# Attention, mixture of experts and feed-forward in one program: the low halves of the first expert's weights computed on VectorE instead of GpSimd

## The chip, the cores and the metric

One core of one Trainium2 chip runs the whole program in one launch. The metric is the device time of that launch in microseconds. The median of three runs of the kernel before is 1288.56 us, the lowest 1285.17 and the highest 1292.94.

## What is computed

Three stages follow each other, each on the output of the one before. Of the reference, shortened:

```python
def _attn_ref(x, state):                  # x (8, 8, 512, 64), state (8, 8, 32, 64)
    xread = softmax(scale * np.matmul(x, state.transpose(0, 1, 3, 2))) @ state
    sread = softmax(scale * np.matmul(state, x.transpose(0, 1, 3, 2))) @ x
    return np.concatenate([xread, sread], axis=2)
def _moe_ref(x, expert_emb, tau, w1, w2): # w1 (8, 512, 1024), w2 (8, 1024, 512)
    expert_idx = np.argmax(xn @ en.T / tau, axis=1)   # rows and embeddings of length one
    for e in range(E):
        mask = expert_idx == e
        h = np.maximum(x[mask] @ w1[e], 0.0)
        out[mask] = gate_w[mask, None] * (h @ w2[e])
def _moe2_ref(x, w_in, w_out, alpha):     # w_in (512, 2048), w_out (2048, 512)
    h = x @ w_in
    g = np.maximum(h, 0.0) + alpha * np.minimum(h, 0.0)
    return g @ w_out
```

Between the stages there are 4352 rows of 512 values: 8 batches of 512 tokens and 32 states.

## The kernel before

All large products after the attention are made with f16 operands in two halves: a matrix v is scaled by a power of two, its high half is v rounded to f16, and its low half is what is left, rounded to f16. A product is then three matmuls: high by high, low by high, high by low. So before the experts' loop starts, the first expert's w1 and w2 must be loaded as f32 (into `st1` and `st2`), measured (sums of squares), scaled, and split into `w1h`, `w1l`, `w2h`, `w2l`.

This is done beside the attention. The attention runs in 16 **units** (k = 0 to 15), one for each batch b and each half g of its heads, written out in order in one Python loop. The order of the instructions on each engine is the order in which this loop records them; nothing reorders it. In unit k:

- TensorE transposes the row maxima (`u_m1T`, line 358), subtracts the maxima (`u_E2T`, line 368), makes the scores of the next unit (`u_S`, line 321), then the products of the states' reading (`u_sread`, line 384), the transposed scores of the next unit (`u_Sn`, line 341), and the products of the tokens' reading (`xr_mm`, line 416), two PSUM tiles of 128 x 584 values.
- ScalarE copies and exponentiates (lines 324, 360, 370, 376), and sums squares.
- VectorE takes the maximum for the next unit (`u_m2`, line 330), scales the states' reading (`u_sr`, lines 395 to 397), reduces the maxima (`u_m1`, lines 350 to 352), does side work that is spread over the units (`put_rows`, line 543: two or three 128 x 128 instructions per unit from unit 7 on; `e_onehot`, lines 492 to 499; `e_scale`, lines 473 to 476), and at the end normalizes the two PSUM tiles (`xr_dve`, lines 436 to 452).
- GpSimd makes a diagonal matrix of the maxima (lines 331 to 334).
- SyncE issues the loads and stores, in order.

The two tiles that line 416 writes have two buffers, so line 384 of a unit waits for the instructions of line 448 of the unit before.

The splitting of the weights hangs on this loop as **tasks**: `tasks[k]` is run near the end of unit k, just after `xr_dve` and one instruction of each chain in `later`. `cv_task(i, c)` splits quarter c of w1 (i = 0, in units 6, 7, 8, 9) or of w2 (i = 1, in units 11, 12, 13, 14), 128 x 1024 values each. Its high half is one ScalarE instruction (`split_hi`, line 130). Its low half is, in the kernel before, four GpSimd instructions: for each of two 512-wide pieces a multiplication by the scale `a_w[i]`, in place in `st1` or `st2` (line 687), and a subtraction (line 688). The later experts' low halves, in the experts' loop, are made by VectorE (`convert`, which calls `split_lo`, line 133).

In unit 14 GpSimd also issues the first two gathers of rows for the experts (`early_load`, line 584), and in unit 15 ScalarE and VectorE split these rows (`early_prep`, lines 130 and 133).

Of the kernel before, what the change touches and what calls it, by code (L numbers as in the profile page):

```python
# [14 lines left out]
ALU = mybir.AluOpType  # L15
# [7 lines left out]
def tile_attn_moe_ffn(ctx, tc, x, xt, state, statet, embt, tau, w1, w2, w_in, w_out, alpha, out):  # L23


    nc = tc.nc
# [71 lines left out]
    a_w = [const.tile([128, 1], F32, name=f"a_w{i}") for i in range(4)]  # L98
# [30 lines left out]
    def split_hi(hi, src, sc):  # L129
        nc.scalar.activation(out=hi, in_=src, func=AF.Copy, scale=sc)  # L130

    def split_lo(lo, hi, src, sc):
        nc.vector.scalar_tensor_tensor(out=lo, in0=src, scalar=sc, in1=hi, op0=ALU.mult, op1=ALU.subtract)  # L133
# [11 lines left out]
    def decode_ops(dst, d):  # L145
# [9 lines left out]
    W = {  # L155
        0: (st1.rearrange("p (c k) f -> p c (k f)", c=4), w1h.rearrange("p (c k) f -> p c (k f)", c=4),
            w1l.rearrange("p (c k) f -> p c (k f)", c=4)),
        1: (st2.rearrange("p (c k) f -> p c (k f)", c=4), w2h.rearrange("p (c k) f -> p c (k f)", c=4),
            w2l.rearrange("p (c k) f -> p c (k f)", c=4)),
    }  # L160
# [41 lines left out]
    def attention(st, pA, pST, pXr):  # L202
# [479 lines left out]
        def cv_task(i, c):  # L682
            def f():
                split_hi(W[i][1][:, c, :], W[i][0][:, c, :], a_w[i])
                for q in range(2):
                    src, hi, lo = (v[:, c, q * 512:(q + 1) * 512] for v in W[i])
                    nc.gpsimd.tensor_tensor(src, src, a_w[i].to_broadcast([128, 512]), ALU.mult)
                    nc.gpsimd.tensor_tensor(lo, src, hi, ALU.subtract)
            return f

        tasks = {k: [] for k in range(2 * B)}
# [33 lines left out]
        for k, (b, g) in enumerate(units):  # L725
# [70 lines left out]
            if k in scales:  # L796
                i = scales[k]
                norm_sum(spare[1][:, 0:4], fsq[i])
                tot = sm.tile([128, 1], F32, tag="sc_t", name="sc_t")
                v = sm.tile([128, 1], I32, tag="sc_v", name="sc_v")  # L800
# [50 lines left out]
        c = B - 1  # L851
# [727 lines left out]
```

## Time and profile before

| | |
|---|---|
| median of 3 runs | 1288.56 us (1285.17 to 1292.94) |
| time of the profiled execution | 1292.34 us |
| its span, first to last instruction | 1290.6 us |
| mean granted TensorE clock | 0.977 of full speed |
| attention (units 0 to 15) | about the first 140 us |
| experts' loop | to about 600 us |
| feed-forward | the rest |

The profile lists five engines: PE is TensorE, DVE VectorE, ACT ScalarE, POOL GpSimd, SP SyncE. A group of instructions is named by source line, engine and operation, what it writes, and what it reads. In a timeline a row begins with the start in us from the span's start and the duration; several like instructions in a row are merged, with their number behind x; in brackets stands how long the engine sat idle before, and which instruction ended that.

### The profile page before, as it was taken

To read this page: it belongs to the slowest core of one execution; us is meant where nothing else is said; L and a number is where in the kernel's file an instruction comes from. 1 tells how busy PE (TensorE), PEld (TensorE's weight loads), DVE (VectorE), ACT (ScalarE), POOL (GpSimd) and SP (SyncE) were. 2 spreads that over 40 slices of the span, in tenths; PEclk is the share of its full clock that TensorE was granted. 3 is DMA by queue.
4 is the path that set the end of the run, shared out by engine and by line. 5 is a ranking of instruction groups with operands and counts; after the bars stand their busy time and mean duration, and the time that the engine had idled before them with its cause. 6 is when DMAs were issued, how large, how long until landed. Compare 5 with 4: busy or idle time off the path is not lost.

```text
span 1290.6 us, 21097 instructions
## 1 busy us (share of the span) xinstructions
PE 1205.5 (93%) x7520; PEld 687.5 (53%) x7520; DVE 810.2 (63%) x1640; ACT 566.1 (44%) x1045; POOL 360.0 (28%) x421
## 2 busy tenths in 40 slices
PE   9887889998888897988999999999999999999997
PEld 5555434443333343333446666666666666666664
DVE  5888856756687776565898555546455454645543
ACT  5955532235484635353555334333343333333343
POOL 2345445554446544454201011020110201001010
PEclk9988989999999998998999999999999999999999
DMA  9884767899999989985102010020101102000000
GB/s 290 273 274 147 208 156 188 185 203 245 205 265 217 274 211 216 181 210 106 38 1 50 18 33 34 2 58 9 34 33 24 43 1 41 25 18 34 1 25 26
DMA packets 221648, 148.48 MB, mean 115 GB/s; under 512 B 174014, under 2 KB 190526, under 8 KB 220480
## 3 DMA queue, kind: packets, MB, share of 16 engines
q1 hardware_dynamic: 210976, 117.30, 38.0%
q0 software_dynamic: 10240, 29.49, 7.5%
q8 instruction: 61, 1.00, 0.3%
q14 instruction: 83, 0.68, 0.2%
q10 hardware_dynamic: 288, 0.02, 0.0%
HBM read 80.13 MB, written 28.40 MB: 84 GB/s over the span
## 4 chain that ended last, share of the span: by engine, by line
PE 52%; DMA 1%; DVE 0%; issue 0%; ACT 0%; POOLq 0%; DVEq 0%
PE bk L1395 27%; PE pm L1449 12%; PE bk L1449 9%; PE bk L1411 2%; PE pm L1411 1%; DMA hT<-hs 1%; PE yp L1066 1%; DMA out_dram<-arena,fr 0%; POOLq L1575 0%; DVE ys L133 0%; DVE arena L1455 0%; DVE ym L1073 0%; ACT arena L1400 0%; ACT ys L130 0%; ACT arena L1368 0%
## 5 line engine op out<-in xcount | busy, mean ns | idle before, releaser
L1395 PE MATMUL bk<-woh,arena 128*128 128x512 f16 x1088 | 399.8, 379 | 0.0
L1395 PEld LDWEIGHTS <-arena 128*128 128x128 f16 x1632 | 158.1, 98 | 100.2
L1395 PE MATMUL bk<-wol,arena 128*128 128x512 f16 x544 | 206.2, 379 | 0.0
L1455 DVE SCALAR_TENSOR_TENSOR arena<-bk,sg,arena 128x256 f32<-128x256 f32 (+1 forms) x128 | 59.7, 466 | 215.4 <-PE bk L1449 215.0
L1457 ACT ACTIVATE arena<-pm,sg 128x256 f32<-128x256 f32 (+1 forms) x192 | 88.4, 461 | 195.6 <-PE pm L1449 194.9
L1066 PE MATMUL yp<-w2h,hT 128*128 128x512 f16 x576 | 140.6, 400 | 29.7 <-DMA hT<-hs 21.4
L1066 PEld LDWEIGHTS <-hT 128*128 128x128 f16 x864 | 83.4, 100 | 138.9 <-DMA hT<-hs 33.9
L1368 ACT CAST arena<-arena 128x512 f16<-128x512 f32 (+1 forms) x144 | 85.1, 591 | 157.8 <-DVE arena L1373 157.4
L1053 PE MATMUL hp<-w1h,xTt 128*128 128x512 f16 x576 | 133.5, 382 | 19.6 <-DMA xTt<-xs 13.4
L1053 PEld LDWEIGHTS <-xTt 128*128 128x128 f16 x864 | 84.5, 98 | 126.1 <-DMA xTt<-xs 15.8
L1284 POOL DMA_INDIRECT gt<-gate_d,fr x34 | 34.3, 1010 | 393.8 <-DMA fr<-y_nat 327.0
L1449 PEld LDWEIGHTS <-wS 128*128 128x128 f16 x1152 | 108.3, 98 | 50.6 <-issue 0.2
L1449 PEld LDWEIGHTS <-winh 128*128 128x128 f16 x1024 | 98.6, 98 | 64.5 <-issue 0.8
L1373 DVE SCALAR_TENSOR_TENSOR arena<-arena,alpha_sb 128x512 f32<-128x512 f32 (+1 forms) x144 | 102.7, 714 | 3.2 <-ACT arena L1415 3.1
L1372 DVE TENSOR_TENSOR arena<-arena 128x512 f16<-128x512 f32 (+1 forms) x144 | 94.0, 658 | 16.1 <-ACT arena L1368 15.1
L130 ACT ACTIVATE ys<-yp,ym 128x512 f16<-128x512 f32 x38 | 26.0, 684 | 172.2 <-DVE ym L1075 155.3
L1449 PE MATMUL pm<-ysum,wS 128*128 128x256 f16 (+1 forms) x768 | 99.6, 266 | 0.1
L1086 POOL DMA_INDIRECT y_nat<-ys,pos x38 | 39.5, 1040 | 209.7 <-issue 151.0
L1295 POOL DMA_INDIRECT out_dram<-arena,fr x34 | 34.7, 1022 | 205.3 <-ACT arena L1400 140.3
L1449 PE MATMUL bk<-yT,winh 128*128 128x256 f16 (+1 forms) x512 | 86.5, 266 | 0.0
L1053 PE MATMUL hp<-w1l,xTt 128*128 128x512 f16 x288 | 68.4, 379 | 0.1
L164 ACT ACTIVATE junk<-st 128x1024 bf16<-128x1024 f32 x56 | 59.2, 1056 | 21.2 <-SPq L1100 8.2
(318 smaller groups left out, 1938.0 us busy)
## 6 DMA issues: line engine op xcount, KB each, us to landing
st<-in_w_dram SPq DMA_DIRECT2D x64, 512.0 KB, 5.8
X<-in_x_dram SPq DMA_DIRECT2D x32, 256.0 KB, 8.8
d<-in_w_in_dram SPq DMA_DIRECT2D x8, 1024.0 KB, 5.6
d<-in_w_out_dram SPq DMA_DIRECT2D x8, 1024.0 KB, 5.4
xs_all<-xrow SPq DMA_DIRECT2D x7, 1056.0 KB, 6.5
xT<-in_xt_dram SPq DMA_DIRECT2D x7, 1024.0 KB, 6.4
xs_all<-xrow SPq DMA_DIRECT2D x2, 528.0 KB, 4.0
xT<-in_xt_dram SPq DMA_DIRECT2D x2, 512.0 KB
```

Of the source, the lines that this page charges most:

```text
L164: nc.scalar.activation(out=junk, in_=W[i][0][:, c, :], func=AF.Square, accum_out=fsq[i][:, c:c + 1])
L1053: nc.tensor.matmul(hp[s][c], lhsT=xTt[s][:, q + k, :], rhs=wt[:, k, c * 512:(c + 1) * 512], start=(i == 0 and k == 0), stop=(i == 2 and k ...
L1066: nc.tensor.matmul(yp[s], lhsT=hT[s][:, q + k, :], rhs=wt[:, k, :], start=(i == 0 and k == 0), stop=(i == 2 and k == KE - 1))
L1086: nc.gpsimd.indirect_dma_start(out=y_nat[:], out_offset=bass.IndirectOffsetOnAxis(ap=pos[:, s:s + 1], axis=0), in_=ys[:].bitcast(I32), in_ ...
L1368: nc.scalar.copy(slot[G[g, m]][:, 0, 0:n], h)
L1372: tt(d[:, 1, 0:n], h, d[:, 0, 0:n], sub)
L1373: return [lambda: nc.vector.scalar_tensor_tensor(h, in0=h, scalar=alpha_sb[:, m:m + 1], in1=h, op0=ALU.mult, op1=ALU.max), hi, lo]
L1395: nc.tensor.matmul(ps, lhsT=slot[G[g, m]][:, lg, t * 128:(t + 1) * 128], rhs=wo[lw][:, m, :], start=(m == order[0] and i == 0), stop=(m == ...
L1411: nc.tensor.matmul(ps, lhsT=wi[l][:, k, m * 128:(m + 1) * 128], rhs=yT[0][:, y + k, :], start=(n == 0), stop=(n == 11))
L1449: nc.tensor.matmul(ps, lhsT=a, rhs=b, start=(i in (1, 2, 5) and j == 0), stop=(j == len(ops) - 1), skip_group_check=True)
L1455: nc.vector.scalar_tensor_tensor(d, in0=ps, scalar=sc, in1=d, op0=ALU.mult, op1=add)
L1457: nc.scalar.activation(out=d, in_=ps, func=AF.Copy, scale=sc)
```

## The change

The four GpSimd instructions of a task give way to one call of `split_lo`, that is one VectorE `scalar_tensor_tensor` over 128 x 1024 values: src times a_w minus hi, written as f16. The staging tiles are no longer scaled in place.

```diff
         def cv_task(i, c):
             def f():
                 split_hi(W[i][1][:, c, :], W[i][0][:, c, :], a_w[i])
-                for q in range(2):
-                    src, hi, lo = (v[:, c, q * 512:(q + 1) * 512] for v in W[i])
-                    nc.gpsimd.tensor_tensor(src, src, a_w[i].to_broadcast([128, 512]), ALU.mult)
-                    nc.gpsimd.tensor_tensor(lo, src, hi, ALU.subtract)
+                split_lo(W[i][2][:, c, :], W[i][1][:, c, :], W[i][0][:, c, :], a_w[i])
             return f
```

Lines below the change move up by three in the file after it.

On VectorE, at the end of unit 9 and the start of unit 10, the order before is this (`xrow`, `lg`: what `xr_dve` writes; `sc_t` to `inv_w`: the scale of w2, a chain in `later`; `m`: the next unit's maximum):

```order
L448 TENSOR_TENSOR lg<-xr,zz 128x64
L436 TENSOR_TENSOR xrow_150<-xr,zz 128x512
L448 TENSOR_TENSOR lg<-xr,zz 128x64
L174 TENSOR_REDUCE sc_t<-xr 128x1
L175 TENSOR_SCALAR sc_v<-sc_t 128x1
L176 TENSOR_SCALAR a_w_106<-sc_v 128x1
L802 RECIPROCAL inv_w_112<-a_w_106 128x1
L330 TENSOR_REDUCE m_1263<-pST 128x1
L395 TENSOR_SCALAR rz_1301<-xr 128x1
```

and with the change this:

```order
L448 TENSOR_TENSOR lg<-xr,zz 128x64
L436 TENSOR_TENSOR xrow_150<-xr,zz 128x512
L448 TENSOR_TENSOR lg<-xr,zz 128x64
L174 TENSOR_REDUCE sc_t<-xr 128x1
L133 SCALAR_TENSOR_TENSOR w1l<-st_122,a_w_105,w1h 128x1024
L175 TENSOR_SCALAR sc_v<-sc_t 128x1
L176 TENSOR_SCALAR a_w_106<-sc_v 128x1
L799 RECIPROCAL inv_w_112<-a_w_106 128x1
L330 TENSOR_REDUCE m_1251<-pST 128x1
L395 TENSOR_SCALAR rz_1289<-xr 128x1
```

The new instruction stands behind the two line 448 instructions and ahead of the next unit's maximum (line 330) and of line 395. There are eight such places, one in each of the units 6 to 9 and 11 to 14.

On GpSimd, in units 6 to 8, the order before is this (`m2b`, `dg`: the diagonal of the maxima):

```order
L331 CAST m2b<-m_964 128x1
L332 TENSOR_TENSOR m2b<-m_964,m2b 128x1
L334 AFFINE_SELECT dg<-m2b 128x256
L687 TENSOR_TENSOR st_122<-st_122,a_w_105 128x512
L688 TENSOR_TENSOR w1l<-st_122,w1h 128x512
L687 TENSOR_TENSOR st_122<-st_122,a_w_105 128x512
L688 TENSOR_TENSOR w1l<-st_122,w1h 128x512
L331 CAST m2b<-m_1055 128x1
```

and with the change this:

```order
L331 CAST m2b<-m_961 128x1
L332 TENSOR_TENSOR m2b<-m_961,m2b 128x1
L334 AFFINE_SELECT dg<-m2b 128x256
L331 CAST m2b<-m_1049 128x1
```

All 32 instructions of lines 687 and 688 are gone from GpSimd; between two units only the three instructions of the diagonal are left.

## Rows read from the trace of the kernel before

**Rows 1.** The page, part 1: busy time, share of the span, instructions of each engine.
```profile
PE 1205.5 (93%) x7520; PEld 687.5 (53%) x7520; DVE 810.2 (63%) x1640; ACT 566.1 (44%) x1045; POOL 360.0 (28%) x421
```

**Rows 2.** Busy time by engine in stretches of 50 to 130 us; granted clock, DMA share.
```profile
core 0: us, PE busy (x) PEld busy (x) DVE busy (x) ACT busy (x) POOL busy (x), PEclk, DMA share, GB/s
...
80.00:90.00 10.00, 7.29 (x52) 5.74 (x52) 7.41 (x30) 4.28 (x13) 1.24 (x4) 0.66 0.89 274
...
120.00:130.00 10.00, 8.74 (x75) 5.76 (x67) 6.93 (x20) 7.04 (x17) 6.41 (x9) 0.71 0.29 84
sum 80.00, PE 64.41 PEld 41.98 DVE 70.03 ACT 50.32 POOL 43.09; mean PE 8.05 PEld 5.25 DVE 8.75 ACT 6.29 POOL 5.39
```

**Rows 3.** Timeline of VectorE and of TensorE where unit 10 begins.
```profile
82.39 0.21 DVE L448 TENSOR_TENSOR lg<-xr,zz 128x64 f32<-128x64 f32 x1
...
82.70 1.99 PE L384 MATMUL xr<-X,E2T 128*64 128x129 f32 x16 [2.97 <-ACT R L310]
```

**Rows 4.** Timeline of VectorE in unit 9, three instructions of its side work.
```profile
77.24 1.06 DVE L543 TENSOR_SCALAR RJ<-io_row,rowf,token 128x128 f32<-128x128 f16 x1
78.22 1.07 DVE L496 TENSOR_TENSOR eq<-Lall,mx 128x64 f32<-128x64 f32 x1
79.22 1.31 DVE L543 TENSOR_SCALAR RJ<-io_row,rowf,token 128x128 f32<-128x128 f16 x1
```

**Rows 5.** Timeline of GpSimd in the same stretch.
```profile
77.04 1.18 POOL L688 TENSOR_TENSOR w1l<-st,w1h 128x512 f16<-128x512 f32 x1
78.18 1.04 POOL L687 TENSOR_TENSOR st<-st,a_w 128x512 f32<-128x512 f32 x1
79.30 1.16 POOL L688 TENSOR_TENSOR w1l<-st,w1h 128x512 f16<-128x512 f32 x1
```

**Rows 6.** Groups by line, VectorE, 50 to 132 us: busy us, mean ns | idle before.
```profile
L543 DVE TENSOR_SCALAR RJ<-io_row,rowf,token 128x128 f32<-128x128 f16 x16 | 15.5, 987 | 0.0
...
L351 DVE CAST m1b<-m 128x16 bf16<-128x16 f32 x9 | 5.0, 561 | 0.3
L352 DVE TENSOR_TENSOR m1b<-m,m1b 128x16 bf16<-128x16 f32 x9 | 4.7, 521 | 0.3
...
L496 DVE TENSOR_TENSOR eq<-Lall,mx 128x64 f32<-128x64 f32 x2 | 2.1, 1075 | 0.0
```

**Rows 7.** The same lines outside: 130.5 to 136 us (line 543) and 18 to 50 us.
```profile
L543 DVE TENSOR_SCALAR RJ<-io_row,rowf,token 128x128 f32<-128x128 f16 x3 | 1.0, 334 | 0.0
...
L351 DVE CAST m1b<-m 128x16 bf16<-128x16 f32 x5 | 1.0, 199 | 0.2
L352 DVE TENSOR_TENSOR m1b<-m,m1b 128x16 bf16<-128x16 f32 x5 | 0.9, 176 | 0.2
L496 DVE TENSOR_TENSOR eq<-Lall,mx 128x64 f32<-128x64 f32 x1 | 0.2, 224 | 0.0
```

**Rows 8.** Line 133 on w1l in the experts' loop: ns minimum/median/maximum, first and last start.
```profile
L133 DVE SCALAR_TENSOR_TENSOR w1l<-st,a_w,w1h x28: 1270/1274/2175, 286.0 to 591.8; 128x1024 f16<-128x1024 f32 x28
```

**Rows 9.** Waits of VectorE, 50 to 131 us: total us, times, longest.
```profile
DVE rz L395 <- PE xr L384: 2.9, 3, 1.4
DVE zz L443 <- PE xr L520: 1.7, 2, 1.3
DVE m L350 <- PE sn L341: 1.2, 4, 0.3
```

**Rows 10.** Timelines: the gathers on GpSimd in unit 14, the rows' split in unit 15.
```profile
125.30 0.97 POOL L584 DMA_INDIRECT X<-xs_all,idx_e  x1 [0.30 <-issue]
...
129.38 1.33 ACT L130 ACTIVATE xe<-X 128x512 f16<-128x512 f32 x2
```

**Rows 11.** Loads of X for unit 10: issue timeline of SP; landing times of two of the four.
```profile
60.55 5.13 SPq L234 DMA_DIRECT2D X<-in_x_dram  x4
...
DMA to landing us min/median/max: 8.9/9.2/9.4
```

**Rows 12.** Busy time in a stretch of the experts' loop, same columns as rows 2.
```profile
200.00:225.00 25.00, 24.61 (x116) 11.11 (x116) 16.97 (x30) 5.57 (x10) 11.69 (x13) 1.00 0.77 179
```

## The prediction

> **What bounds the kernel now.** I read four views in this order. The page's first part gives the shares of the whole span: TensorE busy 93%, VectorE 63%, GpSimd 28% [rows 1]. By these VectorE has room, but the eight tasks all run between 50 and 130 us, so the second view is busy time by stretch: there VectorE is busy 70.03 of 80 us and TensorE 64.41, and TensorE's granted clock falls to a mean of 0.66 at 80 to 90 us and 0.71 at 120 to 130, that is, part of the time at 1.2 GHz [rows 2]. VectorE is the fullest engine of this stretch. The third view, the timelines, shows how a unit hangs together: line 384 of unit 10 starts at 82.70, 0.10 us after VectorE ends the first line 448 of unit 9 (82.39 + 0.21) [rows 3]. The row names another releaser, ACT R, but that was no later. So the circle is: VectorE ends a unit, TensorE makes lines 384, 341 and 416, VectorE runs lines 395 to 397, 350 to 352, the side work, and ends the next. Whatever lengthens VectorE's part lengthens the unit. The fourth view, groups by line, shows that something does: the 16 side instructions of line 543 take 987 ns in the mean between 50 and 132 us, and 334 ns outside [rows 6, 7].
>
> What it is stands in two timelines side by side. Three VectorE instructions in a row end at 78.30, 79.29 and 80.53; the GpSimd instructions of the tasks end at 78.22, 79.22 and 80.46 [rows 4, 5]. Each VectorE instruction ends 0.07 to 0.08 us after one of GpSimd, and the next one is held by the next. The work of the task on GpSimd stops these VectorE instructions for as long as it lasts.
>
> Later the span is TensorE's: in a stretch of the experts' loop it is busy 24.61 of 25 us at full clock [rows 12]. That work waits for the attention's output, so what the attention saves reaches the end.
>
> **The change part by part.** *Added:* eight instructions of line 133 on VectorE. The same shape runs in the experts' loop at a median of 1274 ns [rows 8]. 8 x 1.274 = **+10.2 us** on the fullest engine, all on the circle if nothing hides them. Their high halves come from ScalarE, which is busy 50.32 of 80 us [rows 2] and makes them early in the unit, while VectorE reaches the task at the unit's end: no wait is added. Queued behind the new instruction are lines 330 and 395 of the next unit; GpSimd's diagonal waits for line 330, and is needed a whole unit later.
>
> *Removed:* 32 GpSimd instructions. Their own time is worth nothing, GpSimd bounds nothing here. What is worth something is the stretching. By group, count times (mean within minus mean outside) [rows 6, 7]: line 543, 16 x (987 - 334) = 10.4; line 351, 9 x (561 - 199) = 3.3; line 352, 9 x (521 - 176) = 3.1; line 496, 2 x (1075 - 224) = 1.7. Together **-18.5 us** of VectorE's time. Some smaller groups are left out; against that, a part of line 352's excess may belong to the gathers of unit 14, which stay.
>
> *Waits:* VectorE waits for TensorE 2.9 + 1.7 + 1.2 = 5.8 us in this stretch [rows 9], in units where the clock is low. Two things eat into them. The new instruction stands directly ahead of lines 395 and 350, so it runs while TensorE makes line 384; four of the eight, 5.1 us, stand ahead of the units 8, 10, 12 and 14, where these waits are. And with less stretched side work TensorE idles less between units (2.97 us before line 384 of unit 10 [rows 3]), and may keep its clock. From below, nothing of the 5.8 goes: the waits move but stay. From above, all of it goes. I take **-5.0**, near the upper end, because the first of the two reasons doesn't need the clock.
>
> *Gathers:* GpSimd issues the second at 125.30 behind the diagonal, and ScalarE takes the rows at 129.38, at once when its own queue lets it [rows 10], so up to 129.38 - 125.30 = 4.1 us of transfer lie hidden. Unit 14 gets shorter by more than the issue moves ahead of its end; of the 4.1 us between nothing and 3 us may show. I take **+1.3**.
>
> Loads of X could take the circle over. For unit 10 the last of four is issued by 60.55 + 5.13 = 65.7 and lands about 9.2 later, at 74.9 at the latest; it is needed at 82.70 [rows 11, 3], 7.8 us later. By then I expect some 6.5 us of gain: units 7 to 9 hold about half of the 18.5, against three new instructions (3.8) and with about 1 us of waits. Close, but not late, so it costs nothing; if it is late, that is rival two.
>
> Sum: 10.2 - 18.5 - 5.0 + 1.3 = **-12.0 us**. The profiled execution took 1292.34 us (span 1290.6), so 1280.3 against its own time; it is 3.8 above the median of the runs, 1288.56. Set against that median: **1276.6 us**.
>
> A rule that speaks for a dearer instruction: the Trainium skill, "SBUF — State Buffer", section "SBUF: two separate sides", says that a VectorE instruction with two SBUF inputs, which the new one has, also yields to a GpSimd instruction that reads SBUF, for the whole of that instruction. Line 133's longest case, 2175 ns, is 0.9 over its median [rows 8] and bears that out. If it struck all eight, it would cost 7.2 us and the sum would be -4.8. I leave it out, since the only GpSimd work left here waits for line 330, which VectorE runs behind the new instruction.
>
> **The rivals.** *One, larger gain.* All waits vanish, the clock stays up in the units where it fell, and the gathers arrive in time: -18.5 + 10.2 - 5.8 = -14.1, and TensorE's lines 384 to 416 at 2.4 GHz give up to 3 or 4 more. About -17: 1271.6 us. For it: the low clock of unit 10 comes behind 2.97 us of idling [rows 3], which the stretched side work of the unit before makes. Against it: an engine that waits for VectorE in every unit still idles a little. Chance 0.10.
>
> *Two, the circle changes hands.* VectorE gets its 18.5 us back, but TensorE at 1.2 GHz or the loads of X set the pace of the even units, and the gathers cost 3 us. Of the 8.3 us net (18.5 - 10.2) about half is left, -4: 1284.6 us. For it: the low clock in rows 2, the margin of the loads in rows 11. Chance 0.12, no measurable change.
>
> *Three, slower.* The stretched instructions are long for another reason, say a wait for their own inputs that the profile counts as run time, and keep their length. Then VectorE has only its 10.2 us more; 5.1 fall into waits at most, so +5.1 to +10.2, taken as +7.7: 1296.3 us. It decides from the point where less than about 5 of the 18.5 us come back. For it: VectorE is the fullest engine of the stretch, and work is moved to it from one that is not. The Trainium skill, "Perfetto Trace Analysis", section "Optimizing Scalar/DVE Operations", has this as advice: with a saturated DVE, giving work to GPSIMD may make sense, though between these two it might not help, because they share a port. Against it: the ends in rows 4 and 5, three times within 0.08 us. Chance 0.04.
>
> That the change doesn't do what it says can be ruled out by the order of the instructions: eight more on VectorE, 32 fewer on GpSimd, no other engine's order changed.
>
> **How the numbers follow.** The forecast has 0.74, the rivals 0.10, 0.12 and 0.04. A measurement of this kernel can tell about 0.5% from no change, 6.4 us, so faster means below 1282.1 us. The forecast's own spread is the waits' (0 to -5.8) and the gathers' (0 to +3), -6 to -14 or so, and the runs before spread by 7.8 us among themselves; 0.04 of the forecast and all of rival two lie within 0.5%. Faster 0.80, same 0.16, slower 0.04. The range reaches from rival one with some of the runs' spread, 1268, to rival two, 1284; it leaves out rival three and the edges of the others.
>
> **What would show it.** Right: line 543 on VectorE at 0.33 us in all units, line 351 near 0.2; eight line 133 instructions of about 1.27 us between 50 and 120 us; GpSimd busy some 35 us less; the last attention unit about 12 us earlier, and the same distance at the start of the feed-forward. Wrong: line 543 still near 1 us; line 384 or 395 waiting longer than before, with a granted clock at 0.5 through whole units; line 130 in unit 15 waiting for the gather by more than 3 us; or an earlier attention and an end at the old time.

## The result, and the profile after

Over eleven runs each, the kernel with the change has a median of 1274.75 us (1264.66 to 1282.31), the kernel before 1286.0 us (1280.58 to 1292.94). The ratio is 0.9915, with a 95% interval of 0.989 to 0.994: 11.3 us less in the medians. The forecast was 12.0 us less, 1276.6 us. The profiled execution took 1274.75 us (span 1273.0), that of before 1292.34 (span 1290.6).

The total is close to the forecast, but the profile shows that it came about in another way: the attention's loop gained more than forecast, and lost a good part of that right behind it.

The page of the kernel after, part 1, against [rows 1]:

```profile
PE 1197.9 (94%) x7520; PEld 681.6 (54%) x7520; DVE 793.7 (62%) x1648; ACT 565.4 (44%) x1045; POOL 324.3 (25%) x389
```

GpSimd is busy 35.7 us less, with 32 instructions fewer. VectorE has eight instructions more and is busy 16.5 us less.

The groups of instructions on VectorE by line and shape, after the change, from 50 to 117 us, against [rows 6, 7]. Columns as there: busy us and mean ns behind the first bar, idle time behind the second.

```profile
L133 DVE SCALAR_TENSOR_TENSOR w2l<-st,a_w,w2h 128x1024 f16<-128x1024 f32 x4 | 5.1, 1275 | 0.0
L133 DVE SCALAR_TENSOR_TENSOR w1l<-st,a_w,w1h 128x1024 f16<-128x1024 f32 x4 | 5.1, 1274 | 0.0
L543 DVE TENSOR_SCALAR RJ<-io_row,rowf,token 128x128 f32<-128x128 f16 x16 | 5.1, 339 | 0.0
L352 DVE TENSOR_TENSOR m1b<-m,m1b 128x16 bf16<-128x16 f32 x9 | 1.6, 175 | 0.3
L351 DVE CAST m1b<-m 128x16 bf16<-128x16 f32 x9 | 1.6, 175 | 0.3
...
L496 DVE TENSOR_TENSOR eq<-Lall,mx 128x64 f32<-128x64 f32 x2 | 0.4, 218 | 0.0
```

Read the means. Line 543 takes 339 ns where it took 987, lines 351 and 352 take 175 ns where they took 561 and 521, line 496 takes 218 ns where it took 1075: all are back at the values that they had outside the stretch. The eight new instructions take 1.27 us each.

The same three instructions as in [rows 4], and the new one of the same unit, in VectorE's timeline after the change (start, duration):

```profile
72.88 0.34 DVE L543 TENSOR_SCALAR RJ<-io_row,rowf,token 128x128 f32<-128x128 f16 x1
73.14 0.21 DVE L496 TENSOR_TENSOR eq<-Lall,mx 128x64 f32<-128x64 f32 x1
73.28 0.34 DVE L543 TENSOR_SCALAR RJ<-io_row,rowf,token 128x128 f32<-128x128 f16 x1
...
76.40 1.27 DVE L133 SCALAR_TENSOR_TENSOR w1l<-st,a_w,w1h 128x1024 f16<-128x1024 f32 x1
```

What took 3.3 us in [rows 4] takes 0.7.

**The unit loop.** Unit 6 ends at 54.8 us in both traces (the end of its second line 448). From there to the end of unit 14, busy time by engine, first before, then after:

```profile
55.00:130.80 75.80, 60.08 (x524) 39.60 (x525) 66.49 (x183) 46.63 (x102) 40.32 (x56) 0.86 0.70 215
```

```profile
55.00:110.80 55.80, 51.29 (x520) 32.51 (x522) 53.50 (x190) 44.65 (x99) 8.31 (x26) 1.00 0.88 268
```

The columns are those of [rows 2]. The stretch is 20.0 us shorter. VectorE is busy 66.49 - 53.50 = 13.0 us less, and its idle time falls from 9.3 to 2.3 us, 7.0 less. TensorE's granted clock has a mean of 1.00 where it had 0.86. The end of unit 14, before and after:

```profile
130.60 0.21 DVE L448 TENSOR_TENSOR lg<-xr,zz 128x64 f32<-128x64 f32 x1
```

```profile
110.60 0.21 DVE L448 TENSOR_TENSOR lg<-xr,zz 128x64 f32<-128x64 f32 x1
```

**Unit 15 gives part of it back.** The next landmark is the routing table, which needs the last unit. Its first instruction before and after:

```profile
146.53 0.44 DVE L898 TENSOR_TENSOR pp<-OH,sb 128x272 f32<-128x272 f16 x1
```

```profile
134.43 0.44 DVE L895 TENSOR_TENSOR pp<-OH,sb 128x272 f32<-128x272 f16 x1
```

Only 12.1 of the 20.0 us are left, so unit 15 and what follows it take 7.9 us longer than before. The timelines of four engines in this stretch, after the change (SPq is the queue of SyncE's transfers), show by what:

```profile
109.03 0.83 SPq L482 DMA_DIRECT2D xs_all<-xrow  x1
109.52 0.95 POOL L584 DMA_INDIRECT X<-xs_all,idx_e  x1 [0.30 <-issue]
109.96 0.45 SPq L696 DMA_DIRECT2D st<-in_w_dram  x1
...
111.74 1.22 PE L416 MATMUL xr<-R,E 128*128 128x292 f32 x4 [0.23 <-DVE rk L531]
...
117.95 0.72 ACT L130 ACTIVATE xe<-X 128x512 f16<-128x512 f32 x1 [5.41 <-DMA X<-xs_all,idx_e]
118.71 0.75 DVE L133 SCALAR_TENSOR_TENSOR xe<-X,xe 128x512 f16<-128x512 f32 x1 [5.26 <-ACT xe L130]
120.17 2.31 PE L416 MATMUL xr<-R,E 128*128 128x292 f32 x4 [7.21 <-DVE sr L397]
122.88 2.29 PE L416 MATMUL xr<-R,E 128*128 128x292 f32 x4
```

The second gather is issued at 109.52, between a store of 1056 KB (line 482) and a load of 512 KB (line 696), and its rows are taken at 117.95, 8.4 us later, where [rows 10] showed 4.1. ScalarE waits 5.41 us for them. VectorE waits 5.26 us for ScalarE, with lines 395 to 397 of unit 15 queued behind the wait. TensorE waits 7.21 us for line 397. TensorE's clock falls at 115.0, 2 us into this wait, and rises again at 125.2: behind the wait the same four matmuls of line 416 take 2.3 us instead of 1.22. Of the 10.2 us at 1.2 GHz, TensorE has work in some 5:

```profile
115.00:125.00 10.00, 4.83 (x16) 3.31 (x17) 5.48 (x28) 3.94 (x10) 3.08 (x4) 0.50 0.64 168
```

**Behind the attention.** The experts' loop starts 13.6 us earlier than before (158.8 against 172.4), the feed-forward 17.6 us earlier (610.4 against 628.0), and the feed-forward itself takes 655.9 us in both. So in these two traces the experts' loop is 4.0 us shorter. Its length is no property of either kernel, though: over the profiles below it lies between 447.7 and 462.7 us, for the kernel before at 455.6 and 457.5, for the one after at 451.6 and 447.7, and in two variants of the latter at 455.6 and 455.2. The 12.1 us at the routing table agree with the 11.3 us of the medians, and these 4.0 us are not claimed for the change.

### The profile page after: what moved, and what is told of

Read it like the earlier page. It is cut to its first block, busy times and chain, and to the rows that moved or that the text cites. A ratio compares the mean times of both kernels' runs of the same rounds, so it can differ in the third digit from the quotient of the medians.

```text
span 1273.0 us, 21064 instructions
## 1 busy us (share of the span) xinstructions
PE 1197.9 (94%) x7520; PEld 681.6 (54%) x7520; DVE 793.7 (62%) x1648; ACT 565.4 (44%) x1045; POOL 324.3 (25%) x389
## 4 chain that ended last, share of the span: by engine, by line
PE 55%; DMA 1%; DVE 0%; issue 0%; ACT 0%; POOLq 0%; DVEq 0%
PE bk L1392 27%; PE pm L1446 12%; PE bk L1446 9%; PE yp L1063 2%; PE bk L1408 2%; PE pm L1408 1%; PE hp L1050 1%; DMA hT<-hs 1%; DMA out_dram<-arena,fr 0%; DVE w2l L133 0%; DVE ym L1070 0%; POOLq L1572 0%; DVEq L116 0%; DVE ys L133 0%; DVE arena L1452 0%
## 5 line engine op out<-in xcount | busy, mean ns | idle before, releaser
L1050 PE MATMUL hp<-w1h,xTt 128*128 128x512 f16 x576 | 133.1, 382 | 16.5 <-DMA xTt<-xs 10.3
L1063 PE MATMUL yp<-w2l,hT 128*128 128x512 f16 x288 | 68.1, 378 | 0.0
```

Of the source, the lines that this page charges most:

```text
L1050: nc.tensor.matmul(hp[s][c], lhsT=xTt[s][:, q + k, :], rhs=wt[:, k, c * 512:(c + 1) * 512], start=(i == 0 and k == 0), stop=(i == 2 and k ...
L1063: nc.tensor.matmul(yp[s], lhsT=hT[s][:, q + k, :], rhs=wt[:, k, :], start=(i == 0 and k == 0), stop=(i == 2 and k == KE - 1))
```

## The experiments

The theory under test: GpSimd's instructions stretch those of VectorE, and each end of a unit waits for VectorE. The rival: the stretched instructions are long for another reason, and the gain comes from TensorE's clock or from the loads. A second question came up with the result: what unit 15's loss hangs on.

**e1: the change, and GpSimd instructions beside it that nobody reads** (`dml` is one more tile of 128 x 512 f16 values).

```diff
                 split_lo(W[i][2][:, c, :], W[i][1][:, c, :], W[i][0][:, c, :], a_w[i])
+                for q in range(4):
+                    src, hi = (v[:, c, q % 2 * 512:(q % 2 + 1) * 512] for v in W[i][:2])
+                    nc.gpsimd.tensor_tensor(dml, src, hi, ALU.subtract)
```

> The changed kernel, with GpSimd kept as busy as before beside it: in each of the eight tasks GpSimd also makes four subtractions of 128x512 values (src minus hi) into a tile that nobody reads, some 4.6 us a task. VectorE still makes the low halves, so the output is the same and nothing waits for GpSimd's extra work. Theory (GpSimd's work stops VectorE's instructions while it lasts): line 543 goes back from 0.34 to about 1 us in the mean, the attention's unit 14 ends not at 110.8 us (the changed kernel) but at 130 to 140, and the whole is slower than the kernel before by 0 to 10 us, near 1290. Rival (the gain comes from something else that the four instructions did, their waits on ScalarE or their writing in place): line 543 stays at 0.34, unit 14 ends at 111, the time is the changed kernel's, 1275.

Measured: 1296.72 us, ratio to before 1.0071 (1.0036 to 1.0105), 22 us over the kernel with the change alone. Unit 14 ends at 135.9 us. GpSimd's four new instructions of unit 9, in its timeline, and VectorE's beside them:

```profile
78.82 4.88 POOL L689 TENSOR_TENSOR dml<-st,w1h 128x512 f16<-128x512 f32 x4
```

```profile
80.26 1.05 DVE L544 TENSOR_SCALAR RJ<-io_row,rowf,token 128x128 f32<-128x128 f16 x1
81.24 0.21 DVE L497 TENSOR_TENSOR eq<-Lall,mx 128x64 f32<-128x64 f32 x1
81.37 1.18 DVE L544 TENSOR_SCALAR RJ<-io_row,rowf,token 128x128 f32<-128x128 f16 x1
82.47 0.21 DVE L498 TENSOR_TENSOR eq<-eq,rev 128x64 f32<-128x64 f32 x1
82.61 1.17 DVE L544 TENSOR_SCALAR RJ<-io_row,rowf,token 128x128 f32<-128x128 f16 x1
```

Lines are one lower here, so line 544 is line 543 of the others. A quarter of 4.88 is 1.22 us, so GpSimd's four end at about 80.04, 81.26, 82.48 and 83.70; VectorE's three end at 81.31, 82.55 and 83.78, each 0.05 to 0.08 us behind one of them, as in [rows 4, 5]. Line 497 here (496 of the others) starts at 81.24, about where one of the four ends, and takes 0.21 us, where it took 1.07 in [rows 4]; why it was not held was not followed. The group of line 544 says the same for all sixteen:

```profile
L544 DVE TENSOR_SCALAR RJ<-io_row,rowf,token 128x128 f32<-128x128 f16 x16 | 16.4, 1044 | 0.0
```

No one waits for the results of the added work, and nothing else in the program has changed. The stretching comes from GpSimd's instructions; the rival falls. VectorE now pays for both, the new instructions and the stretching, and the program is slower than before.

In one place of e1, in unit 6, a new instruction runs beside GpSimd's work (VectorE's timeline, then GpSimd's):

```profile
55.41 1.35 DVE L133 SCALAR_TENSOR_TENSOR w1l<-st,a_w,w1h 128x1024 f16<-128x1024 f32 x1
```

```profile
55.76 2.02 POOL L689 TENSOR_TENSOR dml<-st,w1h 128x512 f16<-128x512 f32 x1
```

Line 133 takes 1.35 us there instead of 1.27. It is GpSimd's instruction, which started later, that is held: 2.02 us, where the median of its group is 1.16.

**e5 and e6: the change for w1 alone, and for w2 alone** (against the kernel before; e6 has `i == 1` and `range(2 - 2 * i)`).

```diff
-                for q in range(2):
+                if i == 0:
+                    split_lo(W[i][2][:, c, :], W[i][1][:, c, :], W[i][0][:, c, :], a_w[i])
+                for q in range(2 * i):
```

> Half of the change: w1's four low halves (units 6 to 9) on VectorE, w2's (units 11 to 14) on GpSimd as in the kernel before. Theory (the change is a sum over units, each with its own stretch and its own new instruction): units 7 to 10 as in the changed kernel, so unit 10 ends at 83.0 (91.2 before), then 39.6 us as before, so unit 14 ends at 122 to 124 (130.8 before, 110.8 changed); the gathers find a long unit 14 and stay hidden, line 133's wait on them under 1 us; time 1277 to 1280. Rival (the gain comes only when GpSimd is wholly free): unit 14 ends at 127 or later.

> The other half: w2's four low halves (units 11 to 14) on VectorE, w1's on GpSimd as before. Theory: unit 10 ends at 91.2 as before, then 27.8 us as in the changed kernel, so unit 14 ends at 118 to 120; unit 14 is short now, so the gathers come late as in the changed kernel, line 133 waits 4 to 6 us for them, TensorE 6 to 7, and of the 11.8 us some 4 are left: time 1279 to 1284. Rival (the late gathers are an accident of the changed kernel's times, of the transfers of that moment): no wait, time about 1275.

Measured: e5 1283.73 us, ratio 0.9983 (0.9958 to 1.0007); e6 1285.86 us, ratio 0.9993 (0.9968 to 1.0017). Neither can be told from before. The ends of unit 14 in e5 and e6:

```profile
119.34 0.22 DVE L448 TENSOR_TENSOR lg<-xr,zz 128x64 f32<-128x64 f32 x1
```

```profile
118.80 0.21 DVE L448 TENSOR_TENSOR lg<-xr,zz 128x64 f32<-128x64 f32 x1
```

So each half shortens the unit loop, by 11.2 and 11.8 us. But at the routing table only 4.2 and 4.9 us are left (142.31 and 141.63 against 146.53). What eats the rest shows in the waits of VectorE and TensorE between 50 and 150 us, of e5 and then of e6 (us in total, times, longest):

```profile
DVE xe L133 <- ACT xe L130: 4.5, 2, 3.8
...
PE xr L416 <- DVE sr L397: 5.7, 1, 5.7
```

```profile
DVE xe L133 <- ACT xe L130: 4.2, 2, 2.6
...
PE xr L416 <- DVE sr L397: 5.8, 2, 5.3
```

It is the wait that the whole change has too. I had expected it under 1 us in e5, unit 14's end there at 122 to 124 us (it came at 119.6), and both times lower than they came: misses, and the useful ones. The loss behind the loop is about 7 us already when the loop gains 11 us, and the whole change pays it once (7.9 us), not twice. Each half alone pays it out of half the gain, and looks like nothing. Part of that stays open for e6: the interval of its ratio reaches to 4.1 us less, so the 4.9 us at its table lie outside it, and what takes up the rest behind the table was not followed.

**e2: the low halves left out altogether.** The call of `split_lo` is taken out, and `w1l` and `w2l` are zeroed once by GpSimd at the start.

```diff
+            nc.gpsimd.memset(w1l, 0.0)
+            nc.gpsimd.memset(w2l, 0.0)
...
-                split_lo(W[i][2][:, c, :], W[i][1][:, c, :], W[i][0][:, c, :], a_w[i])
```

> Leaves out the low halves of the first expert's weights (both tiles are set to zero once), on VectorE and on GpSimd, so 8 instructions of 1.27 us less on VectorE than in the changed kernel. Theory (the eight instructions stand on VectorE's circle, so they cost the unit loop what they last, less what TensorE then holds): unit 14 ends at 101 to 106 instead of 110.8. Second theory (the gathers of unit 15 set the attention's end now): the wait of VectorE's line 133 on the gathered rows in unit 15 grows from 5.3 us to 8 or more, and the experts' loop starts only 0 to 5 us earlier than at 158.8. Rival (the eight are hidden): unit 14 ends at 110 or later.

Measured: 1277.64 us, ratio 0.9941 (0.9901 to 0.9982), not faster than the change itself. The experiment has a fault of its own, which shows in GpSimd's timeline:

```profile
12.21 3.51 POOL L283 MEMSET w1l<- 128x4096 f16 x1
15.65 3.54 POOL L284 MEMSET w2l<- 128x4096 f16 x1
```

These two hold up the first units: unit 6 ends at 63.3 us instead of 54.8, and the total says nothing. The unit loop alone can still be read. From the end of unit 6 to that of unit 14 it takes 51.5 us, against 56.0 with the change. Its busy times, in the columns of [rows 2]:

```profile
63.30:114.84 51.54, 49.48 (x513) 32.54 (x512) 46.45 (x183) 44.38 (x99) 8.34 (x26) 1.00 0.83 247
```

So the seven instructions of line 133 in it, 8.9 us by their durations, cost the loop 4.5. VectorE is busy 46.45 us instead of 53.50, only 7.0 less (neighbouring rows of its timeline overlap by some 0.08 us, which is a part of the difference; the rest was not followed). And it is idle 5.1 us instead of 2.3, so 2.8 us of the seven fall into time in which VectorE would else wait. The expected wait of 8 us or more for the gather was 4.6, a miss.

**e3 and e4: the gathers earlier.** e3 issues the two gathers of unit 14 ahead of its line 330; e4 finishes the rows that they need a unit earlier and issues them in unit 13.

```diff
+            if k == KP + 1:
+                early_load()
...
-            if k == KP + 1:
-                early_load()
```

```diff
-        KP = KH + 2
+        KP = KH + 1
...
-                side.append(put_rows(2 + g))
+                side.append(put_rows(4 if k in (KH, KH + 1) else 2 + g))
```

> The changed kernel with the two early gathers recorded ahead of the next maximum's diagonal on GpSimd, in unit 14; nothing else moves. In the changed kernel they go out at 108.2 and 109.5, at the time of a 1056 KB store (109.0) and a 512 KB load (110.0) of SP's queue, and the second lands at 117.9, 8.4 after its issue instead of 4.1. Theory (the gathers set the end of the attention, by their place beside these transfers): issued about 106.1 and 107.4, they land at about 111 to 113, line 133's wait of 5.3 us on them falls below 2, the experts' loop starts 3 to 5 us earlier than at 158.8, time about 1270. Rival (what follows the attention waits for other things, the stall costs nothing): loop start and time as in the changed kernel.

> The changed kernel with the early gathers a whole unit earlier (unit 13): the side work of line 543 in units 11 and 12 is four instructions each instead of three and two, so that the row numbers are there a unit sooner; one more at 0.26 us each, none in unit 13. Theory: the rows are there when unit 15 wants them, the 7.2 us in which TensorE waits in unit 15 (and the 10.2 us at 1.2 GHz behind it) go, unit 14 ends at 110 to 111.5 as before, the experts' loop starts 6 to 8.5 us before 158.8, time about 1267. Rival: as in the run before it.

Measured: e3 1273.23 us, ratio to before 0.9898 (0.9864 to 0.9932); e4 1272.33 us, ratio 0.9898 (0.9851 to 0.9946). The waits shrink or go: in e3 the second gather is issued at 108.19 and taken at 113.65, and VectorE waits 0.8 us; in e4 it is issued at 103.71 and nobody waits. But the table starts at 133.30 and 133.12 us, only 1.1 and 1.3 us earlier than with the change: a miss against what was expected, in both. That is less than two profiles of the changed kernel differ by (134.43 here, 132.94 in e9 below), and the intervals of the three ratios overlap, so neither run can be told from the change. TensorE's timeline in unit 15 of e4 shows why:

```profile
115.67 1.25 PE L416 MATMUL xr<-R,E 128*128 128x292 f32 x4 [1.86 <-DVE sr L397]
...
118.20 2.29 PE L416 MATMUL xr<-R,E 128*128 128x292 f32 x4
```

And the busy time, clock and transfers of the stretch behind it:

```profile
117.00:131.00 14.00, 13.10 (x58) 7.80 (x57) 8.93 (x40) 5.73 (x14) 7.11 (x8) 0.51 0.52 160
```

The wait of 7.21 us is down to idles of 1.86 and 0.91 us, but then the granted clock is 0.51 for 14 us: TensorE runs at 1.2 GHz from 117.2 to 130.9 us, longer than with the change, and is busy 13.10 of the 14 us. In e3 it falls in the same way, from 117.4 to 131.0 us. What the gathers gave, the clock took. So the loss of unit 15 has two parts, the wait and the clock.

**e7: e4, and TensorE kept busy in unit 15** by 22 matmuls into a PSUM tile that nobody reads, 14 behind the first four of line 416 and 8 behind line 659.

```diff
+        def keep(n):
+            kp = pST.tile([128, S], F32, tag="pST", name="kp")
+            for _ in range(n):
+                nc.tensor.matmul(kp[:, 0:256], lhsT=nones, rhs=ones.bitcast(BF16), start=True, stop=True)
...
+                    if ct == ts[0]:
+                        keep(14)
...
+                keep(8)
```

> The kernel with the gathers a unit earlier, and 22 matmuls of 128x256 bf16 values more in unit 15 (14 behind the first four of line 416, 8 behind line 659) whose result nobody reads. In the kernel without them the wait of 7.2 us was gone, and yet routing ended only 1.3 us earlier, since TensorE ran at 1.2 GHz from 117.2 to 130.9. Theory (what the gathers gave was taken back by the clock, and the clock falls because TensorE idles in unit 15, 1.9 and 0.9 us): the granted clock stays at 2.4 GHz, the instruction of line 895 (the routing's table) starts at 127 to 129 instead of 133.1 us, the experts' loop at 152 to 154, time 1264 to 1269. Rival (the clock falls whatever TensorE does there, or the matmuls are in the way): fall as before, table at 133 or later, no gain.

Measured: 1268.88 us, ratio to before 0.9841 (0.9798 to 0.9885), faster than both kernels (its interval lies wholly below that of the change alone, 0.989 to 0.994). TensorE's timeline, and the same window as for e4:

```profile
113.57 1.69 PE L709 MATMUL kp<-ones,nones 128*128 128x256 bf16 x14
115.59 1.25 PE L416 MATMUL xr<-R,E 128*128 128x292 f32 x4 [0.33 <-DVE sr L397]
...
118.10 1.23 PE L416 MATMUL xr<-R,E 128*128 128x292 f32 x4
```

```profile
117.00:131.00 14.00, 12.84 (x117) 8.01 (x115) 13.08 (x60) 7.76 (x18) 9.24 (x10) 1.00 0.79 237
```

The clock is 1.00, and the table starts here:

```profile
128.51 0.44 DVE L903 TENSOR_TENSOR pp<-OH,sb 128x272 f32<-128x272 f16 x1
```

That is 18.0 us earlier than before, at a unit 14 that ends 19.2 us earlier (111.57). The 1.2 us between the two are about what the eighth instruction of line 133 takes, which lies behind the end of unit 14. So with gathers and clock mended, nothing else of the loop's gain is lost in unit 15. This rests on one profile of e7.

**e8 and e9: the kernels before and after, profiled once more.** No edit.

> The kernel before once more, for a second profile: its first profile (1292.34 us) lies 6 us over the median of its runs, 1286.0. Theory (the unit loop repeats, and the experts' loop, which falls to 1.2 GHz at other places in each execution, makes the spread): unit 14 ends at 130.8 within 1 us, the experts' loop starts at 172.4 within 2, and its length differs from 455.6 by several us. Rival (the attention is what spreads): unit 14 ends 3 us or more away from 130.8.

> The changed kernel once more. Theory: unit 14 ends at 110.8 within 0.5 us, line 133 waits 4 to 6.5 us for the gathered rows, the experts' loop starts at 158.8 within 2 us; its length (451.6 before) differs by several us, and with it the time, 1265 to 1282. Rival (the late gathers are one execution's accident): the wait is under 2 us or over 8.

Measured: e8 1291.25 us, e9 1268.95 us. Unit 14 ends at 130.2 and 110.8, the table starts at 145.9 and 132.94: 19.3 us less, then 13.0 less, where the first pair had 20.0 and 12.1; so 6.4 us are lost behind the loop, where it was 7.9. The table of e9:

```profile
132.94 0.44 DVE L895 TENSOR_TENSOR pp<-OH,sb 128x272 f32<-128x272 f16 x1
```

The wait for the gather is there again in e9 (109.54 to 117.25, 7.7 us from issue to use) and not in e8 (124.66 to 128.74, 4.1 us). But TensorE waits 4.18 us in e9 instead of 7.21, and its clock is low in two stretches, 112.3 to 115.7 and 119.1 to 122.6 us, the first of which begins ahead of that wait. How the loss splits between wait and clock thus differs between two executions of the same kernel. e8's experts' loop starts 3.0 us earlier than in the first profile of before, where I had expected 2 at most. The length of that loop is 457.5 and 447.7 us, which moves by several us from execution to execution.

## Why the prediction came out right, and where it did not

**Added, +10.2: right.** Eight instructions at 1274 and 1275 ns. The page of the Trainium skill weighed there, "SBUF — State Buffer", section "SBUF: two separate sides", would have made them dearer if GpSimd had been at work in SBUF when they started; in the changed kernel it is not, and none was longer. The traces agree with the page, by which the one that starts first holds the other: in the experts' loop before, the case of 2174 ns (start 338.4) begins while GpSimd's line 143 runs (337.44 to 339.46), and in unit 6 of e1, where GpSimd's instruction started later, line 133 took 1.35 us and GpSimd's 2.02. What the eight add to the loop is less than they last: e2 has VectorE busy 7.0 us less without seven of them.

**Removed, -18.5: right in mechanism and size.** By the same groups it is 10.4 + 3.5 + 3.1 + 1.7 = 18.7 us: 16 x (987 - 339), 9 x (561 - 175), 9 x (521 - 175), 2 x (1075 - 218). e1 shows the cause: put GpSimd's work back without any use of it, and the stretching is back. "Some smaller groups are left out" hid a little. VectorE's busy time in the loop fell by 13.0 us although seven new instructions were added in it, which by e2 are worth 7.0 us of busy time, so 20.1 us went, 1.6 more than the term. The smaller groups account for it: line 475 (four instructions, 398 to 168 ns) and line 533 (two, 460 to 158 ns) give 1.5 us together, and the four groups themselves 0.2 more than forecast.

**Waits, -5.0: right, a little small.** VectorE's waits for TensorE [rows 9] are nearly gone, and so is one of 1.1 us for ScalarE ahead of line 330; idle time fell by 7.0 us in all. Both reasons given hold: VectorE's idle time in the loop is 9.3 us before, 5.1 in e2, where the clock is at 1.00 and no new instruction stands in the loop, and 2.3 with the change. The case of "one, larger gain", where all waits vanish and the clock stays up, is what the unit loop did. There the forecast's terms, with seven new instructions inside, give 8.9 - 18.5 - 5.0 = -14.6 us, and -20.0 was measured; the 5.4 us between are 1.9 less added, 1.6 more removed and 2.0 more of waits.

**Gathers, +1.3: the step that failed.** "Of the 4.1 us between nothing and 3 us may show" took the transfer time of [rows 10] as it was. It was not. Before, the 1056 KB store of the unit's rows and the 512 KB load went out 3.5 and 4.0 us behind the gather (128.84 and 129.33); now the unit is so short that the gather is issued 0.5 us after the store and 0.4 us ahead of the load, and its rows were taken 8.4 us after the issue. And I priced a late gather by its own wait alone. Behind it VectorE's lines 395 to 397 were queued, behind them TensorE, whose clock fell in this wait, so that it ran on at 1.2 GHz behind it. From the end of unit 14 to the table the forecast has 1.3 for the eighth instruction and 1.3 for the gathers, 2.6; measured is +7.9, and +6.4 in the second pair. In e3 and e4 the wait alone is mended, and the table starts no earlier than in e9. In e7 wait and clock are mended, and it starts at 128.51, 5.9 and 4.4 us ahead of the changed kernel's two profiles. The clock mended alone, with the gather left late, was not tried. The prediction's own test named this sign, a wait of over 3 us for the gather in unit 15.

So two errors of 5.4 and 5.3 us, of opposite sign, cancelled (4.7 and 3.8 in the second pair): the attention ended 12.1 us earlier (13.0), against a forecast of 12.0. The forecast was right for the mechanism of the loop and lucky for the total.

**Same distance at the start of the feed-forward:** 17.6 us in the first pair of traces and 22.3 in the second, not 12. The experts' loop varies by several us with no change in the kernel (e8, e9). Why it does stays open; it was not tried.

**The rivals.** Two, that the circle changes hands, would have left half the net gain: the loads of X were not late, and no unit up to 14 had a lower clock. Three, slower, falls with e1. The advice in the Trainium skill, "Perfetto Trace Analysis", section "Optimizing Scalar/DVE Operations", to move work to GPSIMD when DVE is saturated, has in the same place the doubt that they share a port; here the doubt decides: e1's work on GpSimd, which nobody waited for, cost 22 us.

Open as well: which of the two transfers beside the gather delays it, or whether it is something else of that moment, was not separated. Nor was it tried how few matmuls would do in e7.

## What to carry to other kernels

If an instruction on VectorE has a mean several times that of the same shape elsewhere, lay its timeline beside GpSimd's: ends in lockstep were the sign here that it was being held, and then an offload that looks free is paid for by the engine it was to relieve. When a stage gets shorter by many us, look at each transfer that was just hidden behind it, with the queues it will then be issued beside, and follow the wait through all that is queued behind it, to TensorE's clock at the end. Two halves of a change that each show nothing can be a clear gain together, when a cost behind them is paid once.

## What was not expected of the hardware

- The same gather took 4.1 us from issue to use in [rows 10], 5.5 us in e3, issued at 108.19, and 8.4 us issued at 109.52 beside a store of 1056 KB and a load of 512 KB (7.7 in e9).
- In e4 idles of TensorE of 1.86 and 0.91 us in unit 15 were followed by 13.7 us at 1.2 GHz; in the kernel before, idles of 0.66 and 0.90 us stand in the same two places and the clock stays at 1.00, and so it does in e7, where 22 unread matmuls (1.69 and 1.04 us) fill them.
- Not every instruction of VectorE that ran beside GpSimd's task was stretched. In unit 6 before, GpSimd's four run from 52.15 to 56.66 us. Beside them lines 436 and 448, which read PSUM, took 0.69 and 0.21 us (at 53.25 and 53.85), and lines 528 and 507, reductions of values in SBUF, 0.22 and 0.26 us (at 55.62 and 55.76), each within 0.02 us of what they take with the change; line 533 behind them took 0.76 us, to 56.69, where it takes 0.16 on average with the change.
- A hold goes either way. In e1's unit 6 line 133 ran 1.35 us and GpSimd's instruction beside it 2.02 instead of 1.16 us.
